# Sliding-window attention into routed experts: unit stages issued from one explicit order table

## The chip, the cores and the metric

One core of one Trainium2 chip runs the whole program. The metric is device time in microseconds; three runs of the kernel before gave 190.03, 190.5 and 190.75 us.

## The reference

Two layers, one after the other. Layer one is attention over q, k, v of shape (4 batches, 8 heads, 768, 64) in which a query sees the 8 first keys (the global ones) and the 96 keys up to its own, with a bias that falls by the distance. Layer two takes its output as x of shape (4, 768, 512), gives it to 4 small causal attentions (the experts, width 64), and adds up, for each row, the two experts whose gate is highest.

```python
scores = scale * np.matmul(q, k.transpose(0, 1, 3, 2))
is_global = pos[None, :] < int(n_global)            # 8
is_local = (rel >= 0) & (rel < int(n_local))        # 96
dist = np.where(is_global & ~is_local, float(n_local), np.abs(rel))
scores = np.where(is_global | is_local, scores - slopes[:, None, None] * dist, -1e9)
x = softmax(scores) @ v                             # per head, then heads side by side
...
logits = x @ w_gate                                 # 4 experts, the best 2 are kept
for e in range(E):
    q, k, v = x @ wq[e], x @ wk[e], x @ wv[e]
    a = softmax(where(causal, -1e9, scale * q @ k.T))
    out += weight_of_e * (a @ v @ wo[e])
```

## The kernel before

The work is cut into 24 **units**, u = 0 to 23: a batch (u // 6) and a block of 128 rows in it (u % 6). One unit passes through some 20 stages:

- `load` (L214) brings 128 rows of k, q and v of all heads, 256 KB each, in pieces of 256 bytes; for the first unit of a batch also the 8 global rows of v (L219, four small transfers). `weights_in` and `weights_cast` bring the four weights, one in each of the first four slots.
- `cast` (L224, L228) makes k, q and v 16 bit wide on POOL. `turn` (L235) transposes k, then q, on PE; DVE copies the pair out (L242).
- `local_scores` (L296, L306), twice a unit with four heads each: two bias matmuls through an identity of 128 rows open the score tile, then the scores of head pairs follow. A head has 64 rows, so the two heads of a pair lie in the upper and lower half of PE's array and go into two PSUM banks. ACT takes the exponential out (L309).
- `global_scores` (L276), once for three units, puts the scores of the global keys of all heads into strips of 32 partitions.
- `local_values` (L323, L328): `L323` opens the sum with the global values, one matmul over 128 partitions for each half of the heads; L328 adds the local ones. DVE divides by the row sums (L334, L336).
- `turn_x` (L342), `project_qk` (L357, the k and the q half), `project_v` (L371, which also gives the gate's logits), `route` (the choice of two experts, in seven small steps over three units at a time, on DVE, POOL and ACT; `el` at L481 is its first step on POOL, and waits for DVE's maximum of L477).
- `causal_scores` (L407, up to three a unit, pairs of experts in the two halves of the array; ACT L410), `causal_mask` (POOL L422), `causal_values` (L435), `turn_z` (L452), `output` (L463, copied by ACT at L466, stored at L467).

Nothing is reordered behind the program: each engine does its instructions in the order in which the stages are called, and SP starts the transfers in that order too. That order is a list of 32 slots. Each has a stage and a lag; step s of the loop calls each stage for unit s - lag, so every step is the same pattern over ten units at different depths:

```python
slots = [(5, project_k), (7, route), (7, route), (2, global_scores), (5, project_q), ... (2, ls0)]
for s in range(min(lags), NU + max(lags)):
    for lag, slot in slots:
        if 0 <= s - lag < NU:
            slot(s - lag)
```

PSUM holds two score tiles (`psS`, shared by both attentions and the global scores), one tile for sums of values (`psZ`) and two for everything else (`psT`). Four buffers for each of k, q and v take the loads (`raw`). A last step counts the row sums that are in range and branches to a slower general path if one is not; with these inputs it isn't taken.

Of the kernel before, what the change touches and what calls it, by code (L numbers as in the profile page):

```python
# [19 lines left out]
P = 128  # L20
# [3 lines left out]
def kernel(  # L24
# [179 lines left out]


    fs, qk, gl, ags, xTs, kqs, lgs, wts, a2s, as_, done = ({} for _ in range(11))
    s16s, zs_, x16s, routing, zss, zts, tps, ppss, zs2 = ({} for _ in range(9))

    def load(u):
        b, ri = divmod(u, NT)  # L210
        f = fs[u] = {}
        for nm, src in (("k", k), ("q", q), ("v", v)):
            f[nm] = raw.tile([P, H, Dh], F32, name=nm + "f")
            dma(f[nm][:, :, :],  # L214
                src[b, :, ri * P:(ri + 1) * P, :].rearrange("h j d -> j h d"))
        if ri == 0:
            f["g"] = vgbuf[b % 2]
            for p in range(NP):
                dma(f["g"][32 * p:32 * p + 2 * NG, 0:Dh], v[b, 2 * p:2 * p + 2, 0:NG, :])  # L219

    def cast(u):
        for nm in "kq":
            s16s[nm, u] = pp.tile([P, H, Dh], F16, name="s16", tag="s16", bufs=4)
            G.tensor_copy(s16s[nm, u][:, :, :], fs[u][nm][:, :, :])  # L224
        v16, first = take("vbuf", u)
        if first:
            G.memset(v16[:, :, Dh:VW], 1.0)
        G.tensor_copy(v16[:, :, 0:Dh], fs[u]["v"][:, :, :])  # L228

    def turn(u, i):  # L230

# [12 lines left out]
    def globals_in(u):  # L244

        b, ri = divmod(u, NT)
        if ri == 0:
            kg = pp.tile([P, NP, 32 // NG, NG], F16, name="kg", bufs=2)
            G.tensor_tensor(
                kg[:, :, :, :],  # L250
                kmask[:, :].rearrange("r (a g) -> r a g", g=NG).unsqueeze(1)
                .to_broadcast([P, NP, 32 // NG, NG]),
                qk[u][:, 0, :, 0:NG].unsqueeze(2).to_broadcast([P, NP, 32 // NG, NG]),
                op=Alu.mult)
            vg = pp.tile([P, H, VW], F16, name="vg", bufs=2)
            G.tensor_tensor(vg[:, :, :],
                            fs[u]["g"][:, :].unsqueeze(1).to_broadcast([P, H, VW]),
                            vmask[:, :, :].rearrange("r a b -> r (a b)").unsqueeze(2)
                            .to_broadcast([P, H, VW]), op=Alu.mult)
            gl[b] = (kg, vg)  # L260

    def global_scores(u):

        if u % NH != NH - 1:
            return
        g = u // NH
# [13 lines left out]
        ag = pp.tile([P, NH * P], F16, name="ag", bufs=3)  # L280
        S_.activation(ag[:, :], g_ps[:, :], func=Exp, bias=gbias[:, :], scale=sc1)
        ags[g] = ag

    def local_scores(u, g):

        ri = u % NT
# [6 lines left out]
        s_ps = psS.tile([P, 2, 2, 2 * P], F32, name="sps", tag="s")
        for hh in range(2):
            flat = s_ps[:, hh, :, :].rearrange("r a n -> r (a n)")
            mm(flat[:, 0:2 * w].rearrange("r (a n) -> r a n", a=2),  # L296
               lhsT=ident[:, :], rhs=biasT[:, hh, 2 * g:2 * g + 2, 0:w],
               start=True, stop=False, skip_group_check=True)
        for i in range(2):
            p = 2 * g + i  # L300
            for prev in range(2 if ri else 1):
# [9 lines left out]
                      .rearrange("r h (a n) -> r h a n", a=2), func=Exp, scale=sc1)  # L311
        done[u] = done.get(u, 0) + 1

    def local_values(u, hf):

        b, ri = divmod(u, NT)
        a, ag, vg = held("abuf", u), ags[u // NH], gl[b][1]
        assert done[u] == 2
        c = (ri % NH) * P
# [66 lines left out]
    def route(_):  # L386

        for g in sorted(routing):
            if next(routing[g], "end") != "end":
                return  # L390
# [283 lines left out]
    def part(f, *args):  # L674
        return lambda u: f(u, *args)

    ls0, ls1 = part(local_scores, 0), part(local_scores, 1)
    lv0, lv1 = part(local_values, 0), part(local_values, 1)
    cs0, cs1, cs2 = (part(causal_scores, c) for c in range(3))
    cv0, cv1 = part(causal_values, 0), part(causal_values, 1)  # L680
# [3 lines left out]
    slots = [
        (5, project_k),
        (7, route),
        (7, route),  # L690
        (2, global_scores),
        (5, project_q),
        (5, project_v),
        (4, lv0),
        (4, lv1),
        (5, cs0),
        (0, weights_in),
        (9, turn_z),
        (2, ls1),
        (-2, load),  # L700
        (7, route),
        (7, route),
        (7, route),
        (8, cv0),
        (1, cast),
        (4, turn_x),
        (5, cs1),
        (7, causal_mask),
        (2, weights_cast),
        (7, route),  # L710
        (7, route),
        (1, turn_k),
        (3, globals_in),
        (1, turn_q),
        (8, cv1),
        (9, output),
        (7, route),
        (5, cs2),
        (2, ls0),
    ]  # L720

    lags = [lag for lag, _ in slots]
    for s in range(min(lags), NU + max(lags)):
        for lag, slot in slots:
            if 0 <= s - lag < NU:
                slot(s - lag)
# [65 lines left out]
```

## Time and profile before

| | |
|---|---|
| median of three runs | 190.5 us |
| the profiled execution, whole | 190.69 us |
| its span, first to last instruction | 188.9 us |
| PE busy (matmuls) | 156.4 us, 2486 matmuls |
| DVE, ACT, POOL busy | 107.5, 101.1, 86.7 us |
| HBM read and written | 21.05 and 6.29 MB |

Lines are those of the kernel before, as in the code above. PE is the matrix engine, DVE the vector engine, ACT the scalar engine, POOL GpSimd, SP the engine that starts the transfers. A matmul's busy time runs from its first row to its modelled end, and matmuls overlap; the distance between two starts says more of what one costs. A row of the timeline can stand for several instructions of one kind (x8).

### The profile page before, as it was taken

The numbers are of one execution on the slowest core, as the hardware profiler recorded it, in microseconds if no ns is written. First come the engines' busy times: TensorE is split into PE (matmuls) and PEld (weight loads), VectorE is DVE, ScalarE is ACT, GpSimd is POOL, SyncE is SP. The second block draws the span as 40 slices with busy tenths as digits, with TensorE's granted clock in tenths as the row PEclk, the third lists the DMA queues.
The fourth block names the chain that finished last, engine by engine and source line by source line (L and its number), as shares of the span: only waits on it lengthen the run. The fifth ranks groups of instructions, "written<-read, shape, count | busy, mean of one in ns | idle before, by whom it ended". The sixth has DMA issues, their size and how long they took to land.

```text
span 188.9 us, 6081 instructions
## 1 busy us (share of the span) xinstructions
PE 156.4 (83%) x2486; PEld 109.0 (58%) x2486; DVE 107.5 (57%) x332; ACT 101.1 (54%) x137; POOL 86.7 (46%) x244
## 2 busy tenths in 40 slices
PE   0475299989998999989997999899979999887720
PEld 0232167766756677666674786577648776664400
DVE  5611046655755677557754766567556756775640
ACT  2031324563597565647676555666776567557320
POOL 4537765428913870189107900794078204204300
PEclk9999999999999999999999999999999999999996
DMA  6799999999999579657983977388401110111340
GB/s 131 161 221 218 218 181 254 221 177 220 200 215 257 125 162 186 171 115 167 222 197 68 195 188 170 91 195 205 106 3 56 59 56 3 59 57 59 122 155 19
DMA packets 85651, 27.80 MB, mean 147 GB/s; under 512 B 82288, under 2 KB 82288, under 8 KB 85616
## 3 DMA queue, kind: packets, MB, share of 16 engines
q1 hardware_dynamic: 85616, 27.34, 68.0%
q8 instruction: 21, 0.34, 0.8%
q14 instruction: 14, 0.11, 0.2%
HBM read 21.05 MB, written 6.29 MB: 145 GB/s over the span
## 4 chain that ended last, share of the span: by engine, by line
PE 58%; POOL 10%; DVE 9%; DMA 8%; SPq 5%; issue 5%; ACT 2%; POOLq 0%
PE pps L357 10%; PE sps L296 7%; PE sps L306 5%; PE tp L235 5%; PE zps L435 5%; PE cps L407 5%; PE zps L328 5%; POOL s L224 4%; PE vps L371 4%; PE ops L463 4%; SPq L214 4%; DMA w<-in_moe_wq_dram 3%; PE xps L342 2%; PE zps L323 2%; DVE x L336 2%
## 5 line engine op out<-in xcount | busy, mean ns | idle before, releaser
L410 ACT ACTIVATE a<-cps 128x1024 f16<-128x1024 f32 (+1 forms) x48 | 44.0, 917 | 37.0 <-PE cps L407 36.9
L309 ACT ACTIVATE abuf<-sps 128x892 f16<-128x892 f32 (+1 forms) x48 | 41.4, 862 | 23.2 <-PE sps L306 22.6
L481 POOL TENSOR_TENSOR el<-lg,m 128x12 f32<-128x12 f32 x8 | 1.7, 208 | 68.6 <-DVE m L477 68.6
L235 PE MATMUL tp<-ident,s 128*128 128x128 f16 x192 | 18.1, 235 | 14.7 <-POOL s L224 14.6
L296 PE MATMUL sps<-biasT,ident 128*128 128x446 f16 (+1 forms) x96 | 26.8, 364 | 1.8 <-DVE biasT L75 1.8
L362 DVE CAST kq<-pps 128x512 f16<-128x512 f32 x24 | 16.6, 690 | 20.4 <-PE pps L357 20.4
L242 DVE COPY qkT<-tp 128x1024 f16<-128x1024 f16 x24 | 16.6, 691 | 19.8 <-PE tp L235 19.6
L466 ACT ACTIVATE osb<-ops 128x512 f32<-128x512 f32 x24 | 14.3, 597 | 17.6 <-PE ops L463 7.2
L235 PEld LDWEIGHTS <-s 128*128 128x128 f16 x192 | 12.3, 104 | 18.7 <-POOL s L224 18.1
L306 PEld LDWEIGHTS <-qkT 64*128 64x128 f16 x352 | 9.8, 97 | 18.6 <-issue 17.9
L435 PE MATMUL zps<-v2buf,a 128*128 128x65 f16 x336 | 17.7, 194 | 1.7 <-DVE x L336 1.4
L422 POOL TENSOR_SCALAR_AFFINE_SELECT a<-a 128x256 f16<-128x256 f16 x48 | 18.4, 410 | 0.0
L306 PE MATMUL sps<-qkT 64*128 64x128 f16 (+1 forms) x352 | 18.1, 222 | 0.2 <-DVE qkT L242 0.2
L346 DVE COPY xT<-xps 128x512 f16<-128x512 f16 x24 | 10.2, 425 | 13.7 <-PE xps L342 13.7
L328 PE MATMUL zps<-vbuf,abuf 128*128 128x65 f16 x352 | 17.6, 194 | 0.0
L328 PEld LDWEIGHTS <-abuf 128*128 128x128 f16 x352 | 16.4, 98 | 1.1
L336 DVE TENSOR_TENSOR x<-zps,rinv 128x512 f16<-128x512 f32 x24 | 16.6, 691 | 0.8
L224 POOL CAST s<-kf 128x512 f16<-128x512 f32 x24 | 14.7, 611 | 4.4 <-DMA kf<-in_k_dram 4.3
L435 PEld LDWEIGHTS <-a 128*128 128x128 f16 x336 | 13.5, 97 | 4.2 <-issue 0.7
L224 POOL CAST s<-qf 128x512 f16<-128x512 f32 x24 | 14.8, 616 | 1.8 <-DMA qf<-in_q_dram 1.5
L228 POOL CAST vbuf<-vf 128x512 f16<-128x512 f32 x24 | 14.8, 617 | 1.3 <-DMA vf<-in_v_dram 1.3
L407 PE MATMUL cps<-kq,kq 64*128 64x128 f16 x240 | 15.0, 219 | 0.3 <-DVE kq L362 0.3
(93 smaller groups left out, 263.8 us busy)
## 6 DMA issues: line engine op xcount, KB each, us to landing
kf<-in_k_dram SPq DMA_DIRECT2D x24, 256.0 KB
qf<-in_q_dram SPq DMA_DIRECT2D x24, 256.0 KB
vf<-in_v_dram SPq DMA_DIRECT2D x24, 256.0 KB
out_dram<-osb SPq DMA_DIRECT2D x24, 256.0 KB
w<-in_moe_wk_dram SPq DMA_DIRECT2D x1, 512.0 KB
w<-in_moe_wq_dram SPq DMA_DIRECT2D x1, 512.0 KB
w<-in_moe_wv_dram SPq DMA_DIRECT2D x1, 512.0 KB
w<-in_moe_wo_dram SPq DMA_DIRECT2D x1, 512.0 KB
```

The lines of the kernel that those rows point to most:

```text
L224: G.tensor_copy(s16s[nm, u][:, :, :], fs[u][nm][:, :, :])
L235: nc.tensor.transpose(tps[u][:, i, p, :], s16s["kq"[i], u][:, 2 * p:2 * p + 2, :].rearrange("j h d -> j (h d)"), ident[:, :])
L296: mm(flat[:, 0:2 * w].rearrange("r (a n) -> r a n", a=2), lhsT=ident[:, :], rhs=biasT[:, hh, 2 * g:2 * g + 2, 0:w], start=True, stop=False ...
L306: mm(s_ps[:, hh, :, :].rearrange("r a n -> r (a n)")[:, at:at + n], lhsT=qk[u - prev][r, 0, p, :], rhs=qk[u][r, 1, p, 0:n], start=False, s ...
L309: S_.activation(a[:, :, 2 * g:2 * g + 2, 0:w], s_ps[:, :, :, :].rearrange("r h a n -> r h (a n)")[:, :, 0:2 * w] .rearrange("r h (a n) -> ...
L328: mm(z_ps[:, hq, :], lhsT=a[:, h % 2, h // 2, prev * P:(prev + 1) * P], rhs=held("vbuf", u - prev)[:, h, :], start=False, stop=True, skip_ ...
L336: V.tensor_tensor(x16s[u][:, :, :, :], z4[:, :, :, 0:Dh], rinv.unsqueeze(3).to_broadcast([P, 2, HG, Dh]), op=Alu.mult)
L357: mm(p_ps[:, i, ep, :], lhsT=w[:, ko, ep, :, :].rearrange("r a d -> r (a d)"), rhs=xT[:, ko, :], start=(i == 0 and ep == 0 and ko == 0), s ...
L407: mm(s_ps[:, e2, i, :], lhsT=kqs[b * NT + ci][r, 0, ep, :], rhs=kqs[u][r, 1, ep, :], start=(i == 0), stop=True, skip_group_check=True)
L410: S_.activation(a2[:, :, 4 * c:4 * c + len(part), :], s_ps[:, :, 0:len(part), :], func=Exp, scale=sc2)
L422: G.affine_select(out=d, in_=d, pattern=[[0, NEP], [1, P]], channel_multiplier=-1, base=0, compare_op=Alu.is_ge, fill=0.0)
L435: mm(z_ps[:, e, :], lhsT=a2[:, e % 2, (e // 2) * n + ci, :], rhs=held("v2buf", b * NT + ci)[:, e, :], start=(e == 0 and ci == 0), stop=Tru ...
```

## The change

Four things change in the code.

1. The slots and lags are replaced by a string, `ORDER`, of 700 entries. An entry is a stage of two letters and a number: `tk9` is the turn of k of unit 9, `gs2` the global scores of the third batch of three units. The stages are called in that order, with no period. Each engine's instructions, SP's transfers and POOL's casts among them, follow it.
2. `load` and `cast` are split into k, q and v (`lk`, `lq`, `lv`, `kc`, `qc`, `vc`). `fs` is kept by name and unit, and the 16-bit tiles of k and q have three buffers each instead of four together.
3. The two bias matmuls become a stage of their own, `local_bias` (`ba`, `bb`), which takes the score tile; `local_scores` (`sa`, `sb`) finishes it.
4. The global values become a stage, `global_values` (`vg`). The same two matmuls go over 64 partitions each instead of 128: the first half of the heads has its weights in the partitions 0 to 63 and the second half in 64 to 127, and the rest of each was multiplied with zeros.

`route` now takes its batch of three units by number, and `globals_in` its batch.

```diff
-    def load(u):
-        ...
-        for nm, src in (("k", k), ("q", q), ("v", v)):
-            f[nm] = raw.tile([P, H, Dh], F32, name=nm + "f")
-            ...
+    def load(u, nm):
+        b, ri = divmod(u, NT)
+        f = fs[nm, u] = raw.tile([P, H, Dh], F32, name=nm + "f")
+        dma(f[:, :, :], {"k": k, "q": q, "v": v}[nm][b, :, ri * P:(ri + 1) * P, :]
+            .rearrange("h j d -> j h d"))
+        if nm == "v" and ri == 0:
             for p in range(NP):
...
+    def local_bias(u, g):
+
+        w = W if u % NT else P
+        ss[u, g] = psS.tile([P, 2, 2, 2 * P], F32, name="sps", tag="s")
+        for hh in range(2):
+            mm(ss[u, g][:, hh, :, :].rearrange("r a n -> r (a n)")[:, 0:2 * w]
+               .rearrange("r (a n) -> r a n", a=2),
+               lhsT=ident[:, :], rhs=biasT[:, hh, 2 * g:2 * g + 2, 0:w],
+               start=True, stop=False, skip_group_check=True)
...
+    def global_values(u):
+
+        c = (u % NT % NH) * P
+        ag, vg = ags[u // NH], gl[u // NT][1]
+        zs_[u] = psZ.tile([P, 2, 4 * P], F32, name="zps", tag="z")
+        for hf in range(2):
+            r = slice(hf * Dh, hf * Dh + Dh)
+            mm(zs_[u][:, hf, 0:HG * VW].rearrange("r (h d) -> r h d", h=HG),
+               lhsT=ag[r, c:c + P], rhs=vg[r, hf * HG:(hf + 1) * HG, :],
+               start=True, stop=False, skip_group_check=True)
...
     def local_values(u, hf):
...
-        if hf == 0:
-            zs_[u] = psZ.tile([P, 2, 4 * P], F32, name="zps", tag="z")
         z_ps = zs_[u][:, hf, 0:HG * VW].rearrange("r (h d) -> r h d", h=HG)
-        mm(z_ps, lhsT=ag[:, c:c + P], rhs=vg[:, hf * HG:(hf + 1) * HG, :],
-           start=True, stop=False, skip_group_check=True)
...
-    slots = [
-        (5, project_k),
-        (7, route),
-        ...
-    ]
+    for slot in ORDER.split():
+        stage, *args = stages[slot[:2]]
+        stage(int(slot[2:]), *args)
...
+ORDER = """
+lv0 lk0 lq0 lq1 qc0 kc0 qc1 tk0 lk1 lk2 kc1 tk1 lq2 tq0 tq1 qc2 ba0 kc2 sa0 bb0 sb0 lk3 lq3 lq4
...
+ou19 ou20 za23 tz21 zb23 tz22 ou21 tz23 ou22 ou23
+"""
```

What that does to the engines' own order, at three places. The first is SP, from its first transfer on. Before, it went unit by unit (kf, qf, vf are k, q and v of a unit; w32 a weight):

```order
L214 DMA kf_186<-in_k_dram 128x8x64
L214 DMA qf_188<-in_q_dram 128x8x64
L214 DMA vf_190<-in_v_dram 128x8x64
L219 DMA vgbuf0_180<-in_v_dram 16x1x64 x4
L214 DMA kf_196<-in_k_dram 128x8x64
L214 DMA qf_198<-in_q_dram 128x8x64
L214 DMA vf_200<-in_v_dram 128x8x64
L139 DMA w32_202<-in_moe_wk_dram 128x16x64
```

Now:

```order
L212 DMA vf_186<-in_v_dram 128x8x64
L216 DMA vgbuf0_180<-in_v_dram 16x1x64 x4
L212 DMA kf_192<-in_k_dram 128x8x64
L212 DMA qf_194<-in_q_dram 128x8x64
L212 DMA qf_196<-in_q_dram 128x8x64
L212 DMA kf_209<-in_k_dram 128x8x64
L212 DMA kf_211<-in_k_dram 128x8x64
L212 DMA qf_220<-in_q_dram 128x8x64
L212 DMA kf_255<-in_k_dram 128x8x64
```

v of unit 0 and its global rows moved ahead of k and q; the first weight, eighth before, now stands behind k and q of units 0 to 6 and v of units 0 to 2.

The second place is PE around the global values of a unit, in the middle of the program (vg and ag are the global values and their exponentials, abuf the local ones, sps a score tile, pps the projections). Before, they followed a projection to v and each was followed by local values:

```order
L371 LDWEIGHTS xT_1231
L371 MATMUL vps_1324<-wvg16_128,xT_1231 128x260
L323 LDWEIGHTS ag_1132
L323 MATMUL zps_1333<-vg_1068,ag_1132 128x260
L328 LDWEIGHTS abuf2_155
L328 MATMUL zps_1333<-vbuf7_165,abuf2_155 128x65
```

Now both stand behind the last scores of a unit, and here a projection follows:

```order
L307 LDWEIGHTS qkT_1083
L307 MATMUL sps_1257<-qkT_1123,qkT_1083 128x95
L307 LDWEIGHTS qkT_1083
L307 MATMUL sps_1257<-qkT_1123,qkT_1083 128x95
L322 LDWEIGHTS ag_980
L322 MATMUL zps_1288<-vg_887,ag_980 128x260
L322 LDWEIGHTS ag_980
L322 MATMUL zps_1288<-vg_887,ag_980 128x260
L364 LDWEIGHTS wk16_127
L364 MATMUL pps_1293<-xT_1219,wk16_127 128x128
```

The pair of global values, two matmuls with local values between them before, is now one run of 64-row work with the scores ahead of it (L307 and L322 work on 64 rows, L364 on 128).

The third place is POOL around the first step of the route, `el`. Before, the second batch of three units:

```order
L375 MEMSET v2buf5_171 128x4
L481 TENSOR_TENSOR el_1207<-lg_846,m1_1205 128x12
L486 TENSOR_SCALAR ge_1211<-el_1207 128x12
L487 TENSOR_TENSOR ge_1211<-ge_1211,el_1207 128x12
L224 CAST s16_1221<-kf_751 128x512
L224 CAST s16_1223<-qf_753 128x512
```

Now, the third batch:

```order
L486 TENSOR_TENSOR el_1708<-lg_1255,m1_1676 128x12
L223 CAST s16q_1712<-qf_1399 128x512
L223 CAST s16k_1738<-kf_1478 128x512
L228 CAST vbuf4_162<-vf_1405 128x8x64
L228 CAST vbuf5_163<-vf_1411 128x8x64
L427 AFFINE_SELECT a2_994<-a2_994 128x2x128 x2
```

A cast of q and one of k still follow `el`, but `el` is `ro2` of the table here, and these casts are `qc16` and `kc16`: the table calls `tk16` and `tq16`, which use them, some 25 entries later. Before, the turn of the k cast was four slots on in the same step.

## Rows read from the trace of the kernel before

**Rows 1.** The page, its head and part 1: busy us, share of the span, instructions.
```profile
span 188.9 us, 6081 instructions
PE 156.4 (83%) x2486; PEld 109.0 (58%) x2486; DVE 107.5 (57%) x332; ACT 101.1 (54%) x137; POOL 86.7 (46%) x244
```

**Rows 2.** By stage: length, busy PE, PEld, DVE, ACT, POOL, clock, DMA, GB/s.
```profile
0.00:24.00 24.00, 9.65 (x80) 4.91 (x81) 6.66 (x30) 4.89 (x6) 14.13 (x46) 1.00 1.09 190
24.00:172.00 148.00, 140.11 (x2309) 100.50 (x2306) 94.47 (x273) 90.63 (x123) 68.82 (x186) 1.00 0.68 147
172.00:189.00 17.00, 6.66 (x104) 3.62 (x102) 6.41 (x30) 5.59 (x9) 3.71 (x13) 0.89 0.23 83
```

**Rows 3.** Timeline of PE, 158 to 162 us: start, us, engine, line, out<-in, count.
```profile
158.48 0.59 PE L463 MATMUL ops<-wo,zt 128*128 128x512 f16 x2
158.91 0.54 PE L296 MATMUL sps<-biasT,ident 128*128 128x446 f16 x2
159.39 0.37 PE L306 MATMUL sps<-qkT 64*128 64x128 f16 x8
159.69 0.62 PE L357 MATMUL pps<-xT,wk 128*128 128x128 f16 x8
160.15 0.61 PE L357 MATMUL pps<-xT,wq 128*128 128x128 f16 x8
160.59 0.61 PE L371 MATMUL vps<-wvg,xT 128*128 128x260 f16 x4
161.04 0.27 PE L323 MATMUL zps<-vg,ag 128*128 128x260 f16 x1
161.15 0.40 PE L328 MATMUL zps<-vbuf,abuf 128*128 128x65 f16 x8
161.40 0.27 PE L323 MATMUL zps<-vg,ag 128*128 128x260 f16 x1
161.51 0.40 PE L328 MATMUL zps<-vbuf,abuf 128*128 128x65 f16 x8
161.84 0.34 PE L407 MATMUL cps<-kq,kq 64*128 64x128 f16 x6
```

**Rows 4.** Timeline of PE, its last matmul.
```profile
181.95 0.19 PE L740 MATMUL nps<-good,ones 128*1 128x2 f32 x2 [0.48 <-DVE ones L738]
```

**Rows 5.** Timeline of SP, PE and POOL, 0 to 30 us.
```profile
2.90 2.81 SPq L219 DMA_DIRECT2D vgbuf<-in_v_dram  x4
4.85 0.61 PE L235 MATMUL tp<-ident,s 128*128 128x128 f16 x4 [4.85 <-POOL s L224]
...
23.91 0.93 PE L296 MATMUL sps<-biasT,ident 128*128 128x446 f16 x2
...
26.16 1.44 POOL L159 CAST wvg<-w 128x256 f16<-128x256 f32 x4 [1.37 <-DMA w<-in_moe_wv_dram]
...
27.89 0.82 PE L357 MATMUL pps<-xT,wk 128*128 128x128 f16 x8
28.55 0.61 PE L357 MATMUL pps<-xT,wq 128*128 128x128 f16 x8
29.00 0.61 PE L371 MATMUL vps<-wvg,xT 128*128 128x260 f16 x4
```

**Rows 6.** The page, part 2: GB/s in 40 slices of 4.72 us.
```profile
GB/s 131 161 221 218 218 181 254 221 177 220 200 215 257 125 162 186 171 115 167 222 197 68 195 188 170 91 195 205 106 3 56 59 56 3 59 57 59 122 155 19
```

**Rows 7.** Waits of PE, 24 to 172 us: total us, times, longest.
```profile
PE tp L235 <- POOL s L224: 5.8, 12, 1.0
```

**Rows 8.** Timeline of POOL and PE, 41 to 43 us.
```profile
41.26 0.21 POOL L481 TENSOR_TENSOR el<-lg,m 128x12 f32<-128x12 f32 x1 [4.86 <-DVE m L477]
...
42.07 0.61 POOL L224 CAST s<-kf 128x512 f16<-128x512 f32 x1
...
42.73 0.40 PE L235 MATMUL tp<-ident,s 128*128 128x128 f16 x4 [0.87 <-POOL s L224]
```

**Rows 9.** The page, part 5: busy us, mean ns, idle before.
```profile
L309 ACT ACTIVATE abuf<-sps 128x892 f16<-128x892 f32 (+1 forms) x48 | 41.4, 862 | 23.2 <-PE sps L306 22.6
```

More of the change, by code (lines that the diff above doesn't have):

```diff
@@ L206, with cast @@
     fs, qk, gl, ags, xTs, kqs, lgs, wts, a2s, as_, done = ({} for _ in range(11))
-    s16s, zs_, x16s, routing, zss, zts, tps, ppss, zs2 = ({} for _ in range(9))
-    def load(u):
+    s16s, ss, zs_, x16s, routing, zss, zts, tps, ppss, zs2 = ({} for _ in range(10))
+    def load(u, nm):
         b, ri = divmod(u, NT)
-        f = fs[u] = {}
-        for nm, src in (("k", k), ("q", q), ("v", v)):
-            f[nm] = raw.tile([P, H, Dh], F32, name=nm + "f")
[L214 to L217, printed above, removed]
-            for p in range(NP):
[L219 to L224, printed above, removed]
+        f = fs[nm, u] = raw.tile([P, H, Dh], F32, name=nm + "f")
+        dma(f[:, :, :], {"k": k, "q": q, "v": v}[nm][b, :, ri * P:(ri + 1) * P, :]
+            .rearrange("h j d -> j h d"))
+        if nm == "v" and ri == 0:
+            for p in range(NP):
+                dma(vgbuf[b % 2][32 * p:32 * p + 2 * NG, 0:Dh],
+                    v[b, 2 * p:2 * p + 2, 0:NG, :])
+    def cast(u, nm):
+        f = fs[nm, u]
+        if nm != "v":
+            s16s[nm, u] = pp.tile([P, H, Dh], F16, name="s16" + nm)
+            G.tensor_copy(s16s[nm, u][:, :, :], f[:, :, :])
+            return
         v16, first = take("vbuf", u)
@@ L227, in cast @@
             G.memset(v16[:, :, Dh:VW], 1.0)
-        G.tensor_copy(v16[:, :, 0:Dh], fs[u]["v"][:, :, :])
+        G.tensor_copy(v16[:, :, 0:Dh], f[:, :, :])
     def turn(u, i):
@@ L242, in turn, with globals_in, global_scores @@
         V.tensor_copy(qk[u][:, :, :, :], tps[u][:, :, :, :])
[L244 to L266, printed above, removed]
+    def globals_in(b):
+        u = b * NT
+        kg = pp.tile([P, NP, 32 // NG, NG], F16, name="kg", bufs=2)
+        G.tensor_tensor(
+            kg[:, :, :, :],
+            kmask[:, :].rearrange("r (a g) -> r a g", g=NG).unsqueeze(1)
+            .to_broadcast([P, NP, 32 // NG, NG]),
+            qk[u][:, 0, :, 0:NG].unsqueeze(2).to_broadcast([P, NP, 32 // NG, NG]),
+            op=Alu.mult)
+        vg = pp.tile([P, H, VW], F16, name="vg", bufs=2)
+        G.tensor_tensor(vg[:, :, :],
+                        vgbuf[b % 2][:, :].unsqueeze(1).to_broadcast([P, H, VW]),
+                        vmask[:, :, :].rearrange("r a b -> r (a b)").unsqueeze(2)
+                        .to_broadcast([P, H, VW]), op=Alu.mult)
+        gl[b] = (kg, vg)
+    def global_scores(g):
         u0 = g * NH
@@ L292, in local_scores @@
         w = W if ri else P
[L293 to L297, printed above, removed]
-               start=True, stop=False, skip_group_check=True)
+        s_ps = ss[u, g]
         for i in range(2):
@@ L384, in project_v, with route @@
             routing[g] = top_two(pp, lgs[g], wts[g], "", NH)
[L386 to L390, printed above, removed]
+    def route(g):
+        next(routing[g], None)
     def causal_scores(u, c):
@@ L672, in general_path @@
                     o_sb[:, :])
[L674 to L682, printed above, removed]
-    slots = [
-        (5, project_k),
-        (7, route),
[L690 to L719, printed above, removed]
-    ]
[L722 to L726, printed above, removed]
+    stages = {
+        "lk": (load, "k"), "lq": (load, "q"), "lv": (load, "v"),
+        "kc": (cast, "k"), "qc": (cast, "q"), "vc": (cast, "v"),
+        "wi": (weights_in,), "wc": (weights_cast,), "gi": (globals_in,),
+        "tk": (turn, 0), "tq": (turn, 1), "ba": (local_bias, 0), "bb": (local_bias, 1),
+        "sa": (local_scores, 0), "sb": (local_scores, 1),
+        "gs": (global_scores,), "vg": (global_values,),
+        "va": (local_values, 0), "vb": (local_values, 1), "tx": (turn_x,),
+        "pk": (project_qk, 0), "pq": (project_qk, 1), "pv": (project_v,), "ro": (route,),
+        "ca": (causal_scores, 0), "cb": (causal_scores, 1), "cc": (causal_scores, 2),
+        "ma": (causal_mask,), "za": (causal_values, 0), "zb": (causal_values, 1),
+        "tz": (turn_z,), "ou": (output,),
+    }
+    for slot in ORDER.split():
+        stage, *args = stages[slot[:2]]
+        stage(int(slot[2:]), *args)
     good = const.tile([P, 2], F32)
```

36 lines of the change are left out of this document (33 added, 3 removed).

## The prediction

> **What bounds the kernel now.** I read four things in turn: the page's busy times, the busy time by stage, PE's own sequence in a steady stretch, and the waits. The reader should see first that PE is busy 156.4 of 188.9 us and no other engine over 107.5 [rows 1], and then where: in 24 to 172 us PE is busy 140.1 of 148, before it 9.65 of 24, after it 6.66 of 17 [rows 2]. So there is a start that waits for data, a long stretch in which PE is the bound, and an end of dependent steps.
>
> Busy time overstates a pipelined engine, so I price PE's work by the distance from one start to the next in a stretch where nothing waits [rows 3]. Sixteen 128x128 projections take 160.59 - 159.69 = 0.90, 0.056 each; four of 260 columns 0.45, 0.111 each; two of 512 columns 0.43, 0.215 each; eight 65-column value products 0.25, 0.030 each; one global-value matmul 0.11. The two bias matmuls and what follows them take 0.48, the eight score matmuls after them 0.30. The same eight value matmuls (L328) take 0.25 when a full-array matmul follows (161.15 to 161.40) and 0.33 when a 64-row one follows (161.51 to 161.84). The difference, some 0.09, is the price of **a change of array form** (full array, 64-row pair, 32-column strip). It is paid in the other direction too: eight scores, whose pairs run together, need 2 x (0.055 + 0.040) = 0.19 by columns and take 0.30. I take 0.095 for each change; two bias matmuls are then 0.188 each.
>
> The order of PE in the kernel before, at these prices: 720 matmuls of 128x128, 40.3 us; bias 16.8; 688 value products 20.6; 344 score pairs of both attentions 19.1; projections to v 10.7; global values 48 x 0.11 = 5.3; outputs 10.3; global scores 1.8; and 208 changes of form, 19.8. Together **144.7 us of work**. PE ends at 182.1 [rows 4], so 37.4 us are lost time: 21.0 up to the first projection to v at 29.0, where 8.0 of work is done (the 126 matmuls ahead of it and 14 changes) [rows 5], and 16.4 after it.
>
> **The change part by part.**
>
> *Fewer changes of form.* The table puts scores beside scores and the biases ahead of both. Counted in the listing of PE's instructions, the changes fall from 208 to 135: 73 x 0.095 = **-6.9 us**. Bounds: 0 if PE then waits for others all the time, -8 at 0.11 each.
>
> *Global values in two row tiles.* Two matmuls over 128 rows become two over 64 rows into two PSUM banks, with the same 260 columns. No row shows this very pair; the score pairs are nearest, 64 rows each and two banks, and eight of them take 0.30 where one after the other would need 0.38 plus the change. So I take one duration per pair: 24 x 0.11 = **-2.6 us**; if they don't overlap, 0. [...]
>
> *The start.* SP now issues k and q of seven units and two v ahead of the first weights. Ahead of the v weights stand 19 loads instead of 12, besides two weights in both. DMA moved 181 to 221 GB/s in the slices from 10 to 28 us [rows 6]; at 217, seven loads of 262 KB take 8.5 us. The v weights reached POOL at 26.16 and took 1.44 to cast [rows 5]; now about 34.7, and cast at 36.2. But by then PE has had 20.7 us of work to do instead of 8.0: 344 matmuls with 34 changes stand ahead of that projection. Lost time there is at least 36.2 - 20.7 = 15.5 against 21.0. The k load of unit 0 stands behind one v load and the four small ones that SP takes 2.8 us to issue [rows 5], so the first turn comes some 3.7 us later than 4.85; that is inside the 15.5. The clock is not. The granted clock reads 1.00 from 0 to 24 us [rows 2], but the bias pair at 23.91 lasts 0.93 instead of 0.54, and eight projections take 0.66 at 27.89 and 0.45 right behind [rows 3, 5]. [...] I add 2.0 for it and for short waits: 17.5 lost, **-3.5 us**; bounds -5.5 and 0.
>
> *The route chain on POOL.* In 24 to 172 us PE waits 5.8 us for casts of k and q, 12 times [rows 7]. The place is the same each time: `el` holds POOL until DVE's maximum is there, the cast of the next k stands behind it and two small instructions more, and PE turns that k next: `el` 41.26, cast 42.07, PE 42.73 [rows 8]. In the table the first k or q cast behind `el` is used after 4.7 us of PE's work or more, in each of the five batches of three units that still have one. These 5.8 go, all of them. What is late next: seven score tiles of units 0 to 8 are asked for again 0.2 to 0.8 us of work after they were filled, less than the 0.86 of an activation [rows 9], and k of units 0, 1, 4, 9 and 21 is cast right ahead of its turn. I put 1.5 us on those: **-4.3 us**. Bounds: -5.8, and +4 if each of the 24 units finds a wait of 0.17.
>
> *The end.* The 104 matmuls from 172 on are 5.0 us of work and take 10.1 [rows 2, 4]. The table leaves nine outputs behind the last projection to k instead of six, with more independent work between dependent steps. I count 0, +-2. From PE's last matmul to the end of the span are 6.8 us that nothing here touches; outside the span another 1.8 (190.69 - 188.9).
>
> *SP, DVE, ACT.* Each load waits for its buffer's cast as before. DVE and ACT do the same instructions, 107.5 and 101.1 us; in the 128 us left between start and end neither becomes the bound. 0.
>
> **Sum:** -6.9 - 2.6 - 3.5 - 4.3 = -17.3, against the profiled execution's 190.69: 173.4. That execution is 0.2 above the median of the runs shown, so 173.2; I say **173**.
>
> **The rivals.**
>
> *The waits stay (177.5 to 182).* A fixed order with two score tiles, one value tile and two others gives any late step to all behind it. If the lost time after the first v projection stays 16.4, the result is 173 + 4.3 = 177.5; if each of 24 units also finds 0.17, 182. For: a bias stage now takes a score tile before its scores can run. Against: in [rows 7] PE waits for no activation at all, and the listing shows 2 to 8 us of work between most stages and their users.
>
> [...]
>
> *Slower: the loads don't come fast enough (193.5).* The table asks for 29 loads and three weights, 9.2 MB, before the turn of unit 10, where 32.2 us of work is done. At 217 GB/s they are there by 47, and 15.5 stays the least lost time. If DMA gives 140 they are there at 70: lost 38 instead of 17.5, +20, 193.5. It decides from about 147 GB/s downward. For: slices of 125 and 115 GB/s between 61 and 85 us [rows 6]. Against: 218 and more from 9 to 24 us, when loads were queued.
>
> *Nothing moves (188 to 191).* The changes of form are saved where PE waits anyway, and another engine's chain takes their place. Against: in 24 to 172 us some 134.6 of PE's 148 us are work at these prices, and the table has less of it to do.
>
> **How the numbers follow.** Forecast 0.64; waits stay 0.18; clock 0.07; loads 0.06; nothing 0.05. Low end: no new wait, start at its bound, end 2 better: 173 - 1.5 - 2.0 - 2 - 2.5 (waits that no row names) = 165. High end 182, the top of the first rival. About 2 in 10 lie outside. 0.5%, 0.95 us, is what a measurement of this kernel can tell from no change. Faster 0.91 (the first three and half of the last), same 0.03, slower 0.06.
>
> **What would show it.** In the profile after: the wait of the turn for POOL's casts gone from the steady stretch; a global-value pair taking about 0.11; the first projection to v at 36 to 38; PE's last matmul near 165. Wrong would be: PE waiting for ACT or DVE by more than 5 us after 40; the turns waiting for loads after 50; pairs that take 0.22; a bias pair still lasting 0.9 after 30.

## The result and the profile after

The changed kernel took 168.0 us, the median of four runs from 167.39 to 170.16; the last of these ran in a slower state and is not in the ratio. The kernel before took 190.26 beside it. The ratio is **0.8816, 95% interval 0.8781 to 0.8852**: 22 us faster. The forecast was 173, its range 165 to 182. So sign and size held, and the time is 5 us better than the sum; most of this part is about those 5 us.

The profiled execution took 168.15 us. Its page, head, part 1 and the GB/s of part 2, answers to [rows 1, 6]:

```profile
span 166.4 us, 6056 instructions
PE 142.4 (86%) x2486; PEld 105.4 (63%) x2486; DVE 105.5 (63%) x332; ACT 100.1 (60%) x137; POOL 87.6 (53%) x244
GB/s 64 122 221 218 218 220 200 208 190 235 97 236 206 225 187 211 214 156 257 210 241 282 208 246 144 224 80 217 88 72 66 127 63 4 63 69 180 202 201 10
```

PE has the same 2486 matmuls and is busy 14 us less. The loads now run at 190 to 235 GB/s from 8 to 42 us. By stage (columns as in [rows 2]):

```profile
0.00:24.00 24.00, 11.45 (x125) 6.85 (x125) 7.41 (x33) 7.32 (x9) 12.81 (x39) 1.00 1.02 176
24.00:56.00 32.00, 28.89 (x483) 20.67 (x483) 19.41 (x45) 16.55 (x22) 19.92 (x56) 1.00 1.01 199
56.00:148.00 92.00, 91.86 (x1745) 72.25 (x1740) 70.77 (x221) 67.35 (x93) 51.84 (x138) 1.00 0.68 159
148.00:167.00 19.00, 10.17 (x147) 5.60 (x144) 7.87 (x36) 8.91 (x15) 3.05 (x11) 0.87 0.38 137
```

From 56 to 148 us PE is busy 91.86 of 92, where in the kernel before it was busy 140.1 of 148 in its own long stretch. PE's waits over the whole span (engine, line, what it waited for: us in total, times, longest), the first four of seven rows:

```profile
PE tp L235 <- POOL s16k L223: 13.5, 3, 10.8
PE sps L285 <- ACT abuf L310: 1.1, 3, 0.5
PE tp L235 <- POOL s16q L223: 0.5, 1, 0.5
PE ztps L457 <- DVE zt L461: 0.5, 1, 0.5
```

The first row is the start: one wait of 10.8 for the first k, two more, of 1.2 and 1.5, for later ones. The twelve waits of [rows 7] are gone, and the new ones, for the score tiles' activations, are 1.1 us in all. PE's timeline and that of SP and POOL, at the places that the prediction named:

```profile
2.14 2.81 SPq L216 DMA_DIRECT2D vgbuf<-in_v_dram  x4
4.99 0.41 SPq L212 DMA_DIRECT2D kf<-in_k_dram  x1
10.84 0.61 PE L235 MATMUL tp<-ident,s16k 128*128 128x128 f16 x4 [10.84 <-POOL s16k L223]
15.69 0.92 PE L285 MATMUL sps<-biasT,ident 128*128 128x446 f16 x2
20.82 0.54 PE L285 MATMUL sps<-biasT,ident 128*128 128x446 f16 x2 [0.48 <-ACT abuf L310]
37.22 1.44 POOL L159 CAST wvg<-w 128x256 f16<-128x256 f32 x4 [0.88 <-DMA w<-in_moe_wv_dram]
38.85 0.61 PE L378 MATMUL vps<-wvg,xT 128*128 128x260 f16 x4
41.55 2.62 SPq L216 DMA_DIRECT2D vgbuf<-in_v_dram  x4
41.70 0.27 PE L322 MATMUL zps<-vg,ag 64*128 64x260 f16 x2
41.90 0.40 PE L349 MATMUL xps<-ident,x 128*128 128x128 f16 x4
51.54 0.40 PE L235 MATMUL tp<-ident,s16k 128*128 128x128 f16 x4 [1.46 <-POOL s16k L223]
159.33 0.19 PE L708 MATMUL nps<-good,ones 128*1 128x2 f32 x2 [0.48 <-DVE ones L706]
```

k of unit 0 is issued at 4.99 behind one v load and the four small ones, and its turn comes at 10.84 (4.85 before). A bias pair lasts 0.92 at 15.69 and 0.54 at 20.82: matmuls of 128x128 that follow each other start 0.107 us apart up to 18.3 and 0.056 apart after 20.0 (two bias matmuls 0.356 at 18.3 and 0.188 at 19.0), though the granted clock of the stage reads 1.00. Before, the distance fell from 0.107 to 0.056 at about 28.3. The v weights reach POOL at 37.22, and the first projection to v is at 38.85. A global-value pair starts 0.20 ahead of what follows; by the prices of the prediction that is 0.11, and 0.09 for the change of form. PE's last matmul ends at 159.5 instead of 182.1.

**Where the 22.5 us went.** The prediction's prices, put on every matmul of both kernels, give the lost time at each point, which is the time there less the work of all matmuls ahead. Matmul 2200 is about where the last scores of the kernel before stand:

| stretch (time before; time after) | lost before | lost after | difference | forecast |
|---|---|---|---|---|
| work (all of it) | 144.7 | 135.2 | -9.5 | -9.5 |
| lost up to the first projection to v (29.0; 38.85) | 21.0 | 18.1 | -2.9 | -3.5 |
| from there to 56 us | 2.2 | 2.7 | +0.5 | |
| from 56 us to matmul 2200 of 2486 (159; 140) | 7.2 | 0.4 | -6.8 | -4.3 (this row and the one above) |
| from matmul 2200 to the last | 7.0 | 3.1 | -3.9 | 0 |
| sum | 182.1 | 159.5 | -22.6 | -17.3 |

### The profile page after: what moved, and what is told of

The parts are those of the page before. It is cut to its first block, busy times and chain, and to the rows that moved or that the text cites. A ratio compares the mean times of both kernels' runs of the same rounds, so it can differ in the third digit from the quotient of the medians.

```text
span 166.4 us, 6056 instructions
## 1 busy us (share of the span) xinstructions
PE 142.4 (86%) x2486; PEld 105.4 (63%) x2486; DVE 105.5 (63%) x332; ACT 100.1 (60%) x137; POOL 87.6 (53%) x244
## 4 chain that ended last, share of the span: by engine, by line
PE 49%; SPq 16%; DMA 14%; POOL 7%; issue 6%; DVE 4%; POOLq 0%
SPq L212 12%; PE pps L364 8%; PE zps L440 6%; PE cps L412 5%; PE vps L378 5%; PE sps L285 5%; DMA w<-in_moe_wk_dram 4%; PE ops L468 4%; PE zps L335 4%; DMA vf<-in_v_dram 4%; PE sps L307 4%; DMA kf<-in_k_dram 3%; DMA qf<-in_q_dram 3%; PE tp L235 3%; SPq L216 3%
## 5 line engine op out<-in xcount | busy, mean ns | idle before, releaser
L242 DVE COPY qkT<-tp 128x1024 f16<-128x1024 f16 x24 | 16.4, 688 | 20.2 <-PE tp L235 20.0
L223 POOL CAST s16q<-qf 128x512 f16<-128x512 f32 x24 | 14.7, 614 | 14.2 <-DMA qf<-in_q_dram 12.7
L427 POOL TENSOR_SCALAR_AFFINE_SELECT a<-a 128x256 f16<-128x256 f16 x48 | 18.3, 410 | 7.3 <-ACT a L415 7.3
L235 PE MATMUL tp<-ident,s16k 128*128 128x128 f16 x96 | 10.2, 234 | 13.6 <-POOL s16k L223 13.5
L223 POOL CAST s16k<-kf 128x512 f16<-128x512 f32 x24 | 14.7, 614 | 6.7 <-DMA kf<-in_k_dram 5.2
L307 PEld LDWEIGHTS <-qkT 64*128 64x128 f16 x352 | 9.5, 95 | 11.3 <-issue 9.2
L235 PEld LDWEIGHTS <-s16k 128*128 128x128 f16 x96 | 6.5, 104 | 15.9 <-POOL s16k L223 14.5
L307 PE MATMUL sps<-qkT 64*128 64x128 f16 (+1 forms) x352 | 15.9, 216 | 0.0
L364 PE MATMUL pps<-xT,wq 128*128 128x128 f16 x192 | 15.2, 219 | 0.2
L440 PE MATMUL zps<-v2buf,a 128*128 128x65 f16 x336 | 14.8, 193 | 0.4 <-DVE zs L451 0.2
L335 PEld LDWEIGHTS <-abuf 128*128 128x128 f16 x352 | 13.3, 97 | 2.4 <-issue 0.8
L364 PE MATMUL pps<-xT,wk 128*128 128x128 f16 x192 | 14.6, 219 | 0.0
L378 PE MATMUL vps<-wvg,xT 128*128 128x260 f16 x96 | 14.6, 275 | 0.0
```

The costliest lines, as they stand in the source:

```text
L223: G.tensor_copy(s16s[nm, u][:, :, :], f[:, :, :])
L235: nc.tensor.transpose(tps[u][:, i, p, :], s16s["kq"[i], u][:, 2 * p:2 * p + 2, :].rearrange("j h d -> j (h d)"), ident[:, :])
L307: mm(s_ps[:, hh, :, :].rearrange("r a n -> r (a n)")[:, at:at + n], lhsT=qk[u - prev][r, 0, p, :], rhs=qk[u][r, 1, p, 0:n], start=False, s ...
L335: mm(z_ps[:, hq, :], lhsT=a[:, h % 2, h // 2, prev * P:(prev + 1) * P], rhs=held("vbuf", u - prev)[:, h, :], start=False, stop=True, skip_ ...
L364: mm(p_ps[:, i, ep, :], lhsT=w[:, ko, ep, :, :].rearrange("r a d -> r (a d)"), rhs=xT[:, ko, :], start=(i == 0 and ep == 0 and ko == 0), s ...
L378: mm(v_ps[:, :], lhsT=xT[:, ko, :], rhs=wvg16[:, ko, :], start=(ko == 0), stop=(ko == NK - 1))
```

## The experiments

Each ratio is to the kernel before, run beside it. The changed kernel, run again as the reference of these experiments:

> The changed kernel once more, on the chip of the three below, so that they can be held against it. Expected: 168 us, ratio to the kernel before 0.88.

It measured 168.49 us, 0.8853 (0.8819 to 0.8888).

### Is the work priced right?

**Global values over 128 rows again**, in the changed kernel:

```diff
-               lhsT=ag[r, c:c + P], rhs=vg[r, hf * HG:(hf + 1) * HG, :],
+               lhsT=ag[:, c:c + P], rhs=vg[:, hf * HG:(hf + 1) * HG, :],
```

> The table as it is, but the two global-value matmuls go over all 128 partitions again, as in the kernel before. Theory (a pair in row tiles takes the time of one matmul, and a change of array form costs 0.095 us): each of 24 units pays one matmul of 0.11 more, 2.6 us, and the changes of form rise from 135 to 141, 0.6 us. Expected 3.2 us slower than the changed kernel, since PE waits for nothing else from 56 us on (some of the first units' share is hidden in the start: 2.5 to 3.2). Rival (the pair does not overlap, and the gain came from the order alone): 0 to 0.6 us slower. [...]

171.18 us, 0.8993 (0.8966 to 0.9019): 2.7 more than the reference, within the 2.5 to 3.2 that was expected. Its timeline of PE, the same pair:

```profile
41.61 0.40 PE L321 MATMUL zps<-vg,ag 128*128 128x260 f16 x2
41.85 0.38 PE L348 MATMUL xps<-ident,x 128*128 128x128 f16 x4
```

0.24 to the next start without a change of form, against 0.20 with one.

**The biases put back beside their scores**: in the table, each `ba` and `bb` stands right ahead of its `sa` or `sb`.

```diff
-... lk3 lq3 lq4 lq5 kc3 ba1 tk2 tq2 sa1 ...
+... lk3 lq3 lq4 lq5 kc3 tk2 tq2 ba1 sa1 ...
```

> The table with each bias stage moved to stand right ahead of its scores, as one stage in effect, everything else in its order. The changes of array form rise from 135 to 157. Theory (each change costs 0.095 us and PE is the bound): 22 x 0.095 = 2.1 us slower than the changed kernel, less up to 0.5 that falls in the start. Rival (the bias stages gained by giving PE something to do while it would wait, not by fewer changes): more than 4 us slower, with new waits of PE for ACT or POOL in the steady stretch. Rival (changes of form cost nothing): same.

170.30 us, 0.8941 (0.8914 to 0.8969): 1.8 us for 22 more changes of form, 0.08 each, where 0.095 was said. From 56 to 148 us PE waits there only once, 0.2 us for DVE, so the cost isn't a wait.

**The pair alone, in the kernel before**: both global-value matmuls over 64 rows, together, ahead of the local values.

```diff
+            for h2 in range(2):
+                r = slice(h2 * Dh, h2 * Dh + Dh)
+                mm(zs_[u][:, h2, 0:HG * VW].rearrange("r (h d) -> r h d", h=HG),
+                   lhsT=ag[r, c:c + P], rhs=vg[r, h2 * HG:(h2 + 1) * HG, :],
+                   start=True, stop=False, skip_group_check=True)
         z_ps = zs_[u][:, hf, 0:HG * VW].rearrange("r (h d) -> r h d", h=HG)
-        mm(z_ps, lhsT=ag[:, c:c + P], rhs=vg[:, hf * HG:(hf + 1) * HG, :],
-           start=True, stop=False, skip_group_check=True)
```

> The kernel before, its slots unchanged, with only the global values in two row tiles, both ahead of the local values of a unit. It stands between a projection and local values, both of the full array, so the changes of form rise from 208 to 255. Theory (0.11 us saved and two changes of 0.095 paid by each unit): -2.6 + 47 x 0.095 = 1.8 us slower than the kernel before, 192. Rival (the row tiles alone are a gain, without the table): 2.6 us faster, 187.7. Rival (a change of form costs more than 0.15 us each): over 4 us slower.

192.43 us, 1.0111 (1.0078 to 1.0144): slower by 2.1. Its timeline of PE shows why:

```profile
161.27 0.61 PE L374 MATMUL vps<-wvg,xT 128*128 128x260 f16 x4
161.81 0.29 PE L324 MATMUL zps<-vg,ag 64*128 64x260 f16 x2
162.03 0.66 PE L331 MATMUL zps<-vbuf,abuf 128*128 128x65 f16 x16
```

The projection takes 0.54 to the next start instead of its 0.45, and the pair 0.22 instead of 0.11. Between full-array neighbours the two changes cost more (0.09 and 0.11) than the pair saves (0.11). The same edit is a gain of 2.7 us in the table and a loss of 2.1 in the slots; what differs is the neighbour.

### What was the route's chain on POOL worth?

**Cast at the front of the slots**, in the kernel before, so that no k cast stands behind `el`:

```diff
     slots = [
+        (1, cast),
         (5, project_k),
...
-        (1, cast),
```

> The kernel before with one slot moved: the casts of a step stand ahead of all its route slots, so the route's first POOL step can no longer hold the casts of k and q. Theory (lost time of the kernel before rises by 1.2 us every third step, at that place alone, six to seven times): 7 to 8 us faster than the kernel before, 182.5 to 183.5, and the wait of the turn for casts is gone from 30 to 170 us. By the row of waits that the prediction used it would be 5.8 us. Rival (the turn waits for loads, and the route only happens to stand there): 0 to 2 us faster, and the turns wait for loads instead. Rival (casts at the front of the step delay the route, and the values wait for it): slower.

186.22 us, 0.9782 (0.9741 to 0.9823): only 4.2 faster (4.6 by the two medians). The turn's waits for casts are gone, but a new one came, in two places near 87 and 125 us, some 1.4 us of lost time each. Its timeline at the first (DVE, POOL and PE):

```profile
83.72 1.06 POOL L256 TENSOR_TENSOR vg<-vgbuf,vmask 128x520 f16<-128x520 f32 x1
...
84.33 2.13 DVE L444 TENSOR_TENSOR ce<-rinv,wt 128x4 f32<-128x4 f32 x1
...
84.73 0.61 POOL L224 CAST s<-kf 128x512 f16<-128x512 f32 x1
...
85.28 0.61 POOL L224 CAST s<-qf 128x512 f16<-128x512 f32 x1
...
85.83 0.62 POOL L228 CAST vbuf<-vf 128x512 f16<-128x512 f32 x1
...
86.98 0.28 PE L323 MATMUL zps<-vg,ag 128*128 128x260 f16 x1 [1.20 <-DVE zs L446]
```

`ce` is 4 elements wide and takes 0.16 as a rule. Here it starts while POOL works and ends at 86.46, with POOL's last cast (86.45); `zs` behind it is late, its value tile is kept, and PE waits. So the miss could mean that the chain is worth 4.2, or that it is worth 7 and this edit loses 3. The next run tells them apart.

**The same, with `ce` reading one of its two operands from PSUM** (a second reciprocal, written in PSUM):

```diff
         V.reciprocal(rinv, z_ps[:, :, Hd])
+        V.reciprocal(z_ps[:, :, Hd], z_ps[:, :, Hd])
         ce = pp.tile([P, E], F32, name="ce")
-        V.tensor_mul(ce[:, :], rinv, wts[u // NH][:, ri % NH, :])
+        V.tensor_mul(ce[:, :], z_ps[:, :, Hd], wts[u // NH][:, ri % NH, :])
```

> The kernel before with the casts ahead of the route slots, as in the run that came out 4.6 us faster and not 7 to 8, and with one more edit: DVE's `ce` takes the reciprocal from PSUM, where a second reciprocal puts it (24 more DVE instructions of 0.18 us), so that it reads one operand from SBUF and not two. In the run without this edit `ce` took 2.13 and 2.05 us twice and 0.94 twice, instead of 0.16, while POOL made vg and casts behind each other; PE then waited for the value tile. Theory (DVE's operation on two SBUF operands is held while POOL works): `ce` stays under 0.5 us everywhere, PE's lost time no longer rises by 1.6 us every six units, and the kernel is 2.5 to 4 us faster than without the edit: 182 to 184, ratio 0.957 to 0.967. Rival (the route itself comes later, and the values wait for its weights): `ce` still waits, and the time stays 186.

183.28 us, 0.9619 (0.9593 to 0.9645): 7.3 faster. All 24 `ce` now take 0.16 (view of the tile `ce`: min, median, max in ns, first and last start in us; after it the run without the edit, and the kernel before):

```profile
L445 DVE TENSOR_TENSOR ce<-zps,wt x24: 161/162/164, 49.0 to 172.5; 128x4 f32<-128x4 f32 x24
```

```profile
L444 DVE TENSOR_TENSOR ce<-rinv,wt x24: 161/164/2133, 48.0 to 174.2; 128x4 f32<-128x4 f32 x24
```

```profile
L444 DVE TENSOR_TENSOR ce<-rinv,wt x24: 161/174/416, 50.0 to 179.5; 128x4 f32<-128x4 f32 x24
```

Between matmul 273 (38 us) and matmul 2200 of its PE this kernel loses 1.9 us, where the kernel before loses 9.1. The route's chain was worth 7.2 us, in the kernel before, by itself: `ce` took at most 0.42 there, so the second edit only takes back what the first one cost.

### What sets the start?

The four small loads of a batch's global rows cost SP 2.81 us at 2.14 and 2.62 at 41.55, and PE's turn waits 1.46 at 51.54 for the cast of a k that came late. **All sixteen on ACT's queue**, at the beginning, into four buffers:

```diff
+    for b in range(B):
+        for p in range(NP):
+            S_.dma_start(vgbuf[b][32 * p:32 * p + 2 * NG, 0:Dh], v[b, 2 * p:2 * p + 2, 0:NG, :])
...
-        if nm == "v" and ri == 0:
-            for p in range(NP):
-                dma(vgbuf[b % 2][32 * p:32 * p + 2 * NG, 0:Dh],
-                    v[b, 2 * p:2 * p + 2, 0:NG, :])
```

> The sixteen small loads of global v rows leave SP: ACT starts all of them at the beginning, into four buffers instead of two. SP then issues k of unit 0 some 2.8 us earlier, and isn't held for 2.6 us at 41.6 us. Theory (what is left of lost time in the start, 20.8 us up to 56, is set by the order and time at which SP issues the loads): 2.5 to 4 us faster than the changed kernel, 164 to 165.5, and the lost time at the first projection to v is 15.3 to 16 instead of 18.1. Rival (the start is set by PE's low clock or by the bytes alone): 0 to 1 us faster. Rival (ACT is held at the start and its first exponentials come late): slower.

167.56 us, 0.8798 (0.8766 to 0.8830): 1.0 faster, a miss; its interval meets that of the reference, so even the 1.0 is not shown. The first turn came at 8.08 instead of 10.84, but the rows of its timeline show what took its place:

```profile
2.14 14.23 ACTq L206 DMA_DIRECT2D vgbuf<-in_v_dram  x16
16.40 1.28 ACT L309 ACT_TABLE_LOAD   x1 [16.40 <-DMA qf<-in_q_dram]
...
18.34 0.90 PE L284 MATMUL sps<-biasT,ident 128*128 128x446 f16 x2 [5.49 <-ACT abuf L309]
```

ACT issued for 14.2 us, its first exponential came behind that, and PE waited 5.49 for a score tile. **Only the first batch's four** on ACT, then **the first two batches' eight** (the loop over `b` goes to 1 or 2, and SP keeps the rest), and then, of the latter, **v of unit 0 moved behind q of unit 5** in the table:

> The changed kernel with only the four small loads of the first batch started by ACT; those of the other three batches stay on SP. In the run with all sixteen on ACT, ACT was held until 16.4 us and PE waited 5.5 us for its first exponential, while the turns no longer waited for loads between 42 and 52 us. Theory (SP's order and the time it loses on small loads set the start): ACT is free by 6 us, the first turn comes at 8 as with sixteen, and the lost time at the first projection to v falls from 18.1 to about 16; the second part, 2.5 us between 42 and 53 us where SP issues the small loads of the second batch, stays. Expected 166 to 167, 1.5 to 2.5 us faster than the changed kernel. Rival (the start is set by the low clock): same.

> The same with the small loads of the first two batches on ACT. Theory: both parts go; lost time is about 16 at the first projection to v and not over 17.5 at 56 us. Expected 164 to 165.5, ratio to the kernel before about 0.865, faster than both kernels. Rival (ACT is still held too long by eight, as by sixteen): lost time 18 or more at the first projection to v, 167 to 168.

> The kernel with the small loads of two batches on ACT, and v of unit 0 moved behind q of unit 5 in the table, so that k of unit 0 is SP's first load. The bytes ahead of the first projection to v are the same. Theory (from unit 5 on, the start is set by the bytes ahead): the first turn comes 1 to 1.5 us earlier, and the time is the same as with v first, within 0.5 us. Rival (the first turn sets the start, through PE's clock or the chain of unit 0): 1 to 1.5 us faster.

0.8735 (0.8696 to 0.8774), 0.8698 (0.8656 to 0.8740) and 0.8720 (0.8693 to 0.8746), so 165.7 to 166.4 us by a median of 190.5. The first and the third came out as expected, the second a little above. All three beat both kernels, by 2 to 3 us against the reference, and their intervals don't meet its own; among themselves they can't be told apart. **130 idle matmuls ahead of the program**, in the changed kernel, to see whether the wide distances of PE's first matmuls (0.107 us up to 18.3) set the start:

```diff
+    warm = psT.tile([P, 512], F32, name="warm", tag="t")
+    for _ in range(130):
+        mm(warm[:, 0:P], lhsT=ident[:, :], rhs=ident[:, :], start=True, stop=True)
     for slot in ORDER.split():
```

> The changed kernel with 130 idle 128x128 matmuls of the identity on PE ahead of everything, so that PE works from about 2 to 10 us, before the first k is there; nothing reads their result. Theory (the start is set by the loads): the early matmuls run at the higher clock, lost time at the first projection to v stays within 0.5 of 18.1, and the time is the same within 0.7 us. Rival (the low clock up to about 19 us sets the start): 1.5 to 3 us faster.

0.8850 (0.8816 to 0.8885): no difference. The lost time of these runs, worked out as in the table above:

| run | first turn of k | lost at the first projection to v | lost at 49 to 53 us |
|---|---|---|---|
| the changed kernel | 10.84 | 18.1 | 20.8 |
| its second run | 10.71 | 17.9 | 20.2 |
| idle matmuls first | 10.71 | 18.4 | 21.0 |
| sixteen small loads on ACT | 8.08 | 20.4 | 20.5 |
| four on ACT | 8.18 | 15.0 | 18.0 |
| eight on ACT | 8.15 | 15.9 | 16.7 |
| eight on ACT, v of unit 0 later | 6.95 | 15.9 | 16.8 |

With the idle matmuls PE's turns wait 4.2 us for k in all, the longest wait 2.4, and the lost time at the first projection is 18.4 against 18.1 and 17.9 without them. So they won nothing; more of them were not tried. An earlier first turn, in the last row, changes nothing either: a wait of 1.3 for a score tile takes its place. SP's time for the small loads does count: 2 to 3 us at the first projection, and with the second batch's four gone too, the later rise to 20.8 goes. What is left, 15 to 16, agrees with the prediction's bound of 15.5, worked out from the bytes ahead of the v weights. Fewer bytes ahead of them were not tried.

### Was the end won by the order?

**The last 80 entries in the slots' order**, in the changed kernel; all that stands ahead of them, up to the last scores of unit 23, is unchanged:

```diff
-... bb23 sb23 ro6 ca19 pk21 pq21 ro6 za16 zb16 pk22 pq22 ma18 ... za23 tz21 zb23 tz22 ou21 tz23 ou22 ou23
+... bb23 sb23 ro6 ro6 ro6 ro6 ro6 ro6 ro6 ou13 ou14 ca19 tz15 ... tz21 za22 ma23 zb22 ou21 tz22 za23 zb23 ou22 tz23 ou23
```

> The last 80 entries of the table, those behind the last scores of unit 23, in the order that the slots of the kernel before would give them; all ahead of them as in the changed kernel. PE has 10 more changes of form, 0.9 us. Theory: the end was won by the order of these pieces, which puts other units' work between dependent steps; then PE waits again for DVE's zs, zt and x and for the causal exponentials, 2 to 4 us, lost time from matmul 2200 to the last goes from 3.1 towards the 7.0 of the kernel before, and the kernel takes 171 to 173.5 us, ratio 0.898 to 0.911. Rival: the end is bounded by a chain that the order of these pieces doesn't set, or the gain there came from what was ready earlier; then no more than the 0.9 us of the changes, 168.5 to 169.5, ratio 0.885 to 0.890.

174.59 us, 0.914 (0.910 to 0.918): 5.5 to 6.2 us more than the two runs of the changed kernel by their ratios, above the theory's range and far from the rival's. In the profiles PE's last matmul comes 6.9 later, at 166.2; 0.9 of it are the 10 changes. Counted from the last scores, at 138 to 139 us in both, the lost time to the end is 3.2 us in the changed kernel and 8.5 here. PE's waits from 140 us on, the longest:

```profile
PE ztps L457 <- DVE zs L451: 2.4, 4, 1.0
PE ops L468 <- DVE zt L461: 1.1, 2, 0.7
PE cps L412 <- DVE kq L369: 0.7, 2, 0.3
PE zps L440 <- DVE x L343: 0.5, 1, 0.5
```

and its last units, one after the other:

```profile
160.68 0.28 PE L457 MATMUL ztps<-ident,zs 128*128 128x128 f16 x2 [0.40 <-DVE zs L451]
160.80 0.77 PE L440 MATMUL zps<-v2buf,a 128*128 128x65 f16 x20
161.41 0.59 PE L468 MATMUL ops<-wo,zt 128*128 128x512 f16 x2
162.50 0.28 PE L457 MATMUL ztps<-ident,zs 128*128 128x128 f16 x2 [0.50 <-DVE zs L451]
```

Values, DVE's division, turn, DVE's copy, output: a unit's chain runs nearly alone and takes 1.8 us, with 1.1 of PE's work in it. In the changed kernel two units' chains run into each other there:

```profile
155.44 0.54 PE L440 MATMUL zps<-v2buf,a 128*128 128x65 f16 x12 [0.22 <-DVE zs L451]
155.82 0.27 PE L457 MATMUL ztps<-ident,zs 128*128 128x128 f16 x2
155.93 0.52 PE L440 MATMUL zps<-v2buf,a 128*128 128x65 f16 x12
156.29 0.27 PE L457 MATMUL ztps<-ident,zs 128*128 128x128 f16 x2
156.48 0.60 PE L468 MATMUL ops<-wo,zt 128*128 128x512 f16 x2
```

## Why the prediction was right, and where its sum was off

*Changes of form, -6.9, and row tiles, -2.6: right.* Three runs priced them, with changes added and the tiles taken out or put in: +1.8 for 22 changes, +2.7 for full-array global values in the table, +2.1 for row tiles in the slots (2.6 saved, 47 changes at 0.095 paid). Each is within 0.5 us of what the two prices give.

*The start, -3.5: it measured -2.9, within its bounds, but not for the reason given.* The least lost time was put at 15.5 and 2.0 added for the clock and short waits. The bound was right (15.0 to 15.9 in the three runs that beat the changed kernel), and the sum was near (18.1, 17.5 forecast). But no run shows the 2.0: with idle matmuls ahead the lost time was 18.4. What the runs showed in its place are SP's 2.8 us for four small loads ahead of nearly everything, which are the 2 to 3 us over the bound. The prediction had counted those 2.8 us as hidden inside the 15.5, since it looked at the first turn (which came 6.0 us later than before, where 3.7 was said); they delay every load behind them as well. The kernel before had them too, but behind three loads, and DMA moved 131 and 161 GB/s in its first two slices [rows 6]; now one load stands ahead of them, and the slices show 64 and 122. The v weights came at 37.2, where 34.7 was said. No run put the old order of the loads back, so the -2.9 as a whole is read from the two traces.

*The route's chain, -4.3: right mechanism, too small.* Behind the first projection to v the lost time fell by 6.3 up to matmul 2200, beyond the term's own bound of 5.8. The term took 5.8 from the wait row and gave 1.5 back for new waits. By itself the chain was worth 7.2, and new waits cost next to nothing: 1.1 for score tiles, all before 33 us, and 0.4 lost from 56 us to matmul 2200. Why the wait row was short can be read in the place of [rows 8], on PE's own timeline of the kernel before:

```profile
41.63 0.23 PE L407 MATMUL cps<-kq 64*128 64x128 f16 x2
42.73 0.40 PE L235 MATMUL tp<-ident,s 128*128 128x128 f16 x4 [0.87 <-POOL s L224]
43.30 0.40 PE L235 MATMUL tp<-ident,s 128*128 128x128 f16 x4 [0.17 <-POOL s L224]
```

The row counts idle time from the modelled end of the last matmul, 0.87 and 0.17. From one start to the next, less the work at its price (0.15 for a score pair with a change of form, 0.22 for four turns), the same two waits lose 0.95 and 0.35: 1.30 instead of 1.04. PE's work was priced by starts and its waits by ends, so 0.1 to 0.2 for each of the 12 waits fell between them. Worked out in the same way, the twelve together lose 7.3 us, against 5.8 in the wait row and 7.2 by the run.

*The end, 0 +-2: this step failed.* It was cut at 172 us, where the slices get thin, and there it gave -2.0. But the end begins near 159, where the scores run out and PE waits for DVE's `zs`, `zt` and `x`, and from there the table wins 3.9. PE's waits in the kernel before, from 159 us on, the longest:

```profile
PE ztps L452 <- DVE zs L446: 2.4, 4, 1.0
PE zps L435 <- DVE x L336: 1.1, 2, 0.6
PE ops L463 <- DVE zt L456: 0.5, 2, 0.4
```

In the changed kernel PE waits 0.2 for `zs`, 0.5 for `zt` and nothing for `x` from 140 us on. The prediction saw "more independent work between dependent steps" in the listing and put no price on it. The run with the slots' tail prices it at about 5 us without its changes of form.

*The rivals.* Waits did not stay. The wide distances of PE's first matmuls did not last: 128x128 matmuls start 0.107 us apart only up to 18.3, where before it was up to about 28.3, although PE began 6 us later. The loads came at 214 GB/s, the mean of the slices from 8 to 42 us (217 was said). The result lies between the forecast and the range's low end, for two of the reasons that the low end was built from: no new waits, and a better end.

*The signs.* The pair takes 0.11, and behind 40 us PE waits for no engine by more than 5 us. Three signs came out otherwise: the first projection to v is at 38.85 (36 to 38 was said); one turn still waits 1.46 at 51.54 for a k that came late, and turns waiting for loads after 50 were named as a sign of being wrong; and PE's last matmul is at 159.3, not near 165.

*Slips in the working, without effect on the sum.* 173 + 4.3 is 177.3 and not 177.5. The 19 loads ahead of the v weights hold three loads of v, where the sentence says two. And 80 of the 344 score pairs have 95 columns: at the prediction's own 0.040 for them the work is 1.2 less, in both kernels alike.

Summed up, the profiled execution is 5.2 us under the sum of 173.4: 3.9 by the end and 2.0 by the chain and the waits that did not come (-6.3 from the first projection to v to matmul 2200, -4.3 forecast), less 0.6 by the start.

## What to carry to other kernels

Price a pipelined engine's work and its waits by the same measure, from start to start, and add them up along the program: the steps in the lost time show a wait's whole price and where the end begins, which busy shares and wait rows do not. Cutting an operation to half the array paid here only where its neighbours had the same form (2.7 us won in the table, 2.1 lost in the slots), so order the work by form first and count the changes. And ask what the order alone can give: the chain's 7.2 us, a third of the gain, came in the periodic order too, with one slot moved and one operand in PSUM. What the runs put down to the table is 73 fewer changes of form, the pair that they make pay, and the end.

## What had not been expected of the hardware

A DVE operation of 128x4 with two operands in SBUF took 0.94 to 2.13 us instead of 0.16, four times in 24, in the run with the casts ahead of the route. The one of 2.13 began while POOL made `vg`, lasted through the three casts behind it, and ended with the last of them (86.46 and 86.45). With one operand in PSUM it took 0.16 all 24 times. That POOL's work held it is read from these rows and runs; by what means was not shown.

ACT was held 14.2 us by starting sixteen loads of 4 KB, 0.9 each; SP took 2.81 for four, and 0.41 for the load of 256 KB behind them.

What stays open: why the runs with four to eight small loads on ACT lose another 0.7 to 1.5 us between 50 and 145 us, where the changed kernel loses 0.4.
